# Starting a fused attention and feed-forward kernel with the value projection from scaled rows, and adding the shift's share at the end

## The chip, the cores and the metric

The kernel runs on one core of a Trainium2 chip. The metric is device time in microseconds (us) from the first to the last instruction of one execution, measured around the program. Before the change it is 832.6 us (median of 4 runs, 831.9 to 833.6). The profile is one further execution, recorded by the hardware profiler; its span is a little shorter than the time of that run (831.0 us in a run of 832.8). Runs here agree within about 0.3%, so differences of a microsecond are looked at in the trace and compared as ratios between runs of the same rounds on the same chip.

The engines are named as the profile names them: PE is the matmul engine (TensorE), DVE is VectorE, ACT is ScalarE, POOL is GpSimd, SP issues most of the DMA loads.

## The reference, cut to what matters

```python
x = A_x                                           # 2048 rows of 1024, bfloat16
mod = (silu(c) @ w_mod).reshape(1, 6, 1, 1024)     # c is one row; w_mod is 1024 x 6144
sa, ca, ga, sb, cb, gb = mod[:, 0], ..., mod[:, 5]

h = layernorm(x) * (1 + ca) + sa                   # scale and shift per column
q, k, v = split(h @ wqkv)                          # 32 heads of 32
phi(t) = where(t > 0, t + 1, exp(t)) + 1e-6
kv = einsum('bhsd,bhse->bhde', phi(k), v)          # summed over all rows
z  = einsum('bhsd->bhd', phi(k))
o  = (phi(q) @ kv) / (phi(q) . z + 1e-6)
x  = x + ga * (o @ wo)
# then the same with sb, cb, gb around a SwiGLU feed-forward block of width 3584
```

The algebra that the change uses: with the scaled rows alone, hs = layernorm(x) * (1 + ca), the values are v = hs @ wv + sa @ wv. The second term is one row, the same for every row of x. Its share in kv is z times that row, so it can be added once, at the end.

## The kernel before

The 2048 rows are worked in four chunks of 512 rows (`sc` 0 to 3), each of four row tiles of 128. Per chunk the kernel computes K, V and Q with 512-column matmuls. After the first two of the eight K groups of the next chunk comes a block `kvp` of 128 narrow matmuls that adds phi(k) times v of the chunk before. Chunk 0 is special: scale and shift must first be computed from `w_mod`. The start, shortened:

```python
for st in range(STC - 1):            # row tiles 0 to 2
    load_x(st, nc.sync)
for k in range(DC // MP):            # scale and shift weights, 8 loads of 384 KB
    load_a(k, 1, nc.scalar if k == 0 else nc.sync)
    load_a(k, 0, nc.sync)
...                                  # wk, the rest of w_mod, wv, row tiles 4 to 7, wq
with in_order(nc.vector, nc.scalar, nc.gpsimd):
    ...                              # statistics, row matvec for scale and shift, transposes
    k_mms(0, gs, accs, 0, 5)         # K of chunk 0 starts here
    ...
    k_evac(0, gs, accs)              # phi on ACT and DVE, frees the accumulators
    k_evac(0, gs7, accs7)
    k_evac(0, gs8, accs8)
for sc in range(NSC):
    if sc > 0:
        k_phase(sc, 0, 2); kv_phase(sc - 1); k_phase(sc, 2, 4); ...
    v_phase(sc)
    if sc + 1 < NSC:                 # layernorm of the next chunk's four row tiles
        with tc.issue_after(last_on[nc.vector.engine] if sc == 0 else last_phi[-5].ins):
            ln1(sc + 1)
    if sc == 0:
        q_phase(0, 0, 6)
```

```python
def phi_to(dst, acc):                # evacuation of one K or Q accumulator
    e = ep.tile([P, NB], BF16, name="eb")
    nc.scalar.activation(out=e[:], in_=acc, func=ACT.Exp)
    nc.vector.tensor_scalar(out=e[:], in0=e[:], scalar1=1.0, scalar2=PHI_EPS, op0=ALU.min, op1=ALU.add)
    last_phi[0] = nc.vector.scalar_tensor_tensor(out=dst, in0=acc, scalar=0.0, in1=e[:], op0=ALU.max, op1=ALU.add)

def ln1_stats(sc, t):                # statistics of one row tile: needs the tile in SBUF
    x_sb = x_tiles.pop(sc * STC + t)
    mv = small.tile([P, STC, 2], F32, name="mv")
    bn(x_sb, mv[:, 0, :])            # two bn_stats and one bn_aggr on DVE
    rstd = rstd_of(mv, 1)
    return sc, t, x_sb, mv, rstd
```

There are four accumulators of the kind that `acc_a()` hands out, and a matmul group that uses one can only start when one is free: in the changed kernel PE waits 3.23 us for one. The order of instructions on each engine is decided by a scheduler when the kernel is built; `issue_after` and `in_order` restrict it. At run time DVE works through its list in order: in the changed kernel it stands idle for 3.82 us with finished work behind the wait.

## Time and profile before

| before | value | view |
|---|---|---|
| time | 832.6 us (831.9 to 833.6) | 4 runs |
| PE busy | 99% of the span | busy table |
| PE share of the chain of waits | 97% | chain |
| first K matmul | 15.59 us | timeline of PE |
| Q of chunk 0 starts | 44.49 us | timeline of PE |
| granted PE clock | 1.00 from 5.8 us on | clock records |

These lines are the busy row of the engines and the chain of work that ended last, by engine and by line (before). "L98" is the helper through which nearly all matmuls go.

```profile
PE 819.9 (99%) x4502; PEld 378.9 (46%) x4581; DVE 344.5 (41%) x659; ACT 168.5 (20%) x253; POOL 64.3 (8%) x166
...
PE 97%; DMA 2%; issue 1%; DVE 0%; ACTq 0%; SPq 0%
```

PE is the bound. The only part of the chain that is not PE lies at the start. This is the chain in order of time, before (columns: start in us, length in us, what):

```profile
1.33 6.07 DMA wme<-in_w_mod_dram
...
7.83 6.40 DMA wme<-in_w_mod_dram
...
14.28 0.51 PE mod_ps L98 x8
14.79 4.21 PE acc L98 x19
```

So the first 14.2 us wait for `w_mod`. After that PE does not pause. The timeline of PE, before (start, length, engine, line, operation, out<-in, shapes, count; a bracket would tell an idle time and what ended it):

```profile
15.59 6.64 PE L98 MATMUL acc<-wk,hT 128*128 128x512 bf16 x29
...
30.68 13.98 PE L98 MATMUL acc<-wv,hT 128*128 128x512 bf16 x63
44.49 13.98 PE L98 MATMUL acc<-hT,wq 128*128 128x512 bf16 x62
```

K, V and Q of chunk 0 follow each other without a bracket. Later, behind the second `kvp`, the line is

```profile
92.25 10.46 PE L98 MATMUL acc<-wk,hT 128*128 128x512 bf16 x47 [0.16 <-issue]
```

that is, K of chunk 2 goes on to its end without a gap above 0.16 us.

What DVE does while they run, before:

```profile
28.49 0.29 DVE L296 TENSOR_SCALAR eb<-eb 128x512 bf16<-128x512 bf16 x1 [2.74 <-ACT eb L295]
28.81 0.69 DVE L298 SCALAR_TENSOR_TENSOR pk<-acc,eb 128x512 bf16<-128x512 f32 x1
...
35.78 0.69 DVE L298 SCALAR_TENSOR_TENSOR pk<-acc,eb 128x512 bf16<-128x512 f32 x1
36.39 1.87 DVE L224 BATCH_NORM_STATS2 stats<-x_sb 128x6 f32<-128x512 bf16 x3
```

The eight evacuations of K (`pk<-acc,eb`) come first, and only then the statistics (`BATCH_NORM_STATS2`) of the next chunk's row tiles.

### The profile page before, as it was taken

How to read it: one execution, taken by the hardware profiler on the slowest of the kernel's cores; microseconds unless marked ns; L12 is line 12 of the kernel's file. 1: busy time of each engine (PE TensorE's matmuls, PEld its weight loads, DVE VectorE, ACT ScalarE, POOL GpSimd, SP SyncE). 2: the span in 40 equal slices, each digit the busy share in tenths (PEclk: the TensorE clock that was granted, in tenths of full speed). 3: DMA queues.
4: the chain of work that ended last, by engine and by line, in shares of the span. 5: the costliest groups of instructions: out<-in, count | busy, mean ns of one | idle time of the engine just before them, and what ended most of it. 6: DMA issues, size and time to landing. Idle time of an engine off the chain costs nothing.

```text
span 831.0 us, 11112 instructions
## 1 busy us (share of the span) xinstructions
PE 819.9 (99%) x4502; PEld 378.9 (46%) x4581; DVE 344.5 (41%) x659; ACT 168.5 (20%) x253; POOL 64.3 (8%) x166
## 2 busy tenths in 40 slices
PE   8999999999999999999999999999999999999998
PEld 4444444444444444444444444444444444444444
DVE  5758879786354335421111354111114431111122
ACT  3455343434111111101111010111111101111000
POOL 2101020120221101100000010000001100000000
PEclk9999999999999999999999999999999999999999
DMA  9893964149986735646343183763405529710011
GB/s 324 296 203 65 194 150 102 37 101 326 375 204 219 227 121 169 160 153 211 110 146 108 54 221 92 249 195 100 153 1 174 152 68 345 231 45 0 19 58 51
DMA packets 144100, 129.07 MB, mean 155 GB/s; under 512 B 58608, under 2 KB 124656, under 8 KB 143536
## 3 DMA queue, kind: packets, MB, share of 16 engines
q1 hardware_dynamic: 139968, 114.97, 46.8%
q0 software_dynamic: 3792, 12.98, 4.9%
q8 instruction: 36, 0.59, 0.3%
q10 hardware_dynamic: 288, 0.40, 0.1%
q14 instruction: 16, 0.13, 0.0%
HBM read 101.98 MB, written 12.72 MB: 138 GB/s over the span
## 4 chain that ended last, share of the span: by engine, by line
PE 97%; DMA 2%; issue 1%; DVE 0%; ACTq 0%; SPq 0%
PE acc L98 90%; PE a_ps L98 7%; DMA wme<-in_w_mod_dram 2%; PE kvp L98 1%; PE wf L98 0%; PE den L98 0%; PE mod_ps L98 0%; ACTq L126 0%; PE tp L101 0%; SPq L135 0%; DVE e L698 0%; DVE ob L701 0%
## 5 line engine op out<-in xcount | busy, mean ns | idle before, releaser
L98 PE MATMUL acc<-h2T,wgu 128*128 128x512 bf16 x1755 | 385.6, 379 | 1.9
L98 PEld LDWEIGHTS <-wgu 128*128 128x128 bf16 x1792 | 175.3, 98 | 211.3
L677 DVE TENSOR_TENSOR gu<-acc,e 128x512 bf16<-128x512 f32 x112 | 77.4, 691 | 289.9 <-PE acc L98 278.8
L98 PE MATMUL acc<-wd,gu 128*128 128x512 bf16 (+2 forms) x908 | 195.2, 372 | 0.9
L676 ACT ACTIVATE e<-acc 128x512 f32<-128x512 f32 x112 | 66.9, 597 | 374.8 <-PE acc L98 363.4
L98 PEld LDWEIGHTS <-gu 128*128 128x128 bf16 x924 | 89.3, 98 | 104.4
L98 PEld LDWEIGHTS <-hT 128*128 128x128 bf16 x512 | 49.6, 98 | 59.8 <-DVE hT L237 0.9
L698 DVE TENSOR_TENSOR e<-acc,gb_bc 128x512 f32<-128x512 f32 (+2 forms) x33 | 22.3, 675 | 131.5 <-PE acc L98 122.5
L98 PE MATMUL a_ps<-wo,pq 128*128 128x512 bf16 x250 | 56.9, 379 | 0.3
L98 PE MATMUL acc<-wk,hT 128*128 128x512 bf16 x251 | 56.4, 379 | 0.5 <-issue 0.3
L98 PE MATMUL acc<-hT,wq 128*128 128x512 bf16 x249 | 55.8, 379 | 0.7 <-issue 0.5
L98 PE MATMUL acc<-wv,hT 128*128 128x512 bf16 x249 | 55.5, 379 | 0.4
L295 ACT ACTIVATE eb<-acc 128x512 bf16<-128x512 f32 x64 | 37.9, 596 | 75.4 <-PE acc L98 73.3
L234 ACT ACTIVATE xn<-x,nmr,rstd 128x1024 bf16<-128x1024 f32 x16 | 19.9, 1241 | 126.0 <-POOL nmr L232 126.0
L98 PEld LDWEIGHTS <-pq 128*128 128x128 bf16 x256 | 25.0, 98 | 30.2
L645 POOL DMA_DIRECT2D x_scratch<-x x16 | 9.8, 615 | 373.8 <-DVE x L638 373.6
L98 PEld LDWEIGHTS <-wq 128*128 128x128 bf16 x256 | 24.6, 98 | 29.8 <-issue 0.9
L296 DVE TENSOR_SCALAR eb<-eb 128x512 bf16<-128x512 bf16 x64 | 18.3, 290 | 31.2 <-ACT eb L295 31.0
L218 POOL TENSOR_TENSOR rstd<-veps,neg_half 128x1 f32<-128x1 f32 x32 | 17.8, 557 | 102.3 <-DVE veps L216 92.3
L638 DVE TENSOR_TENSOR x<-a_ps,x_sb 128x512 f32<-128x512 f32 x32 | 22.1, 690 | 8.6 <-PE a_ps L98 7.9
L701 DVE TENSOR_TENSOR ob<-e,x1r 128x512 bf16<-128x512 f32 (+2 forms) x33 | 22.3, 675 | 1.0
L639 DVE BATCH_NORM_STATS2 stats<-x 128x6 f32<-128x512 f32 x32 | 22.1, 693 | 1.0
(92 smaller groups left out, 295.9 us busy)
## 6 DMA issues: line engine op xcount, KB each, us to landing
wgu<-in_B_w_gate_dram SPq DMA_DIRECT2D x28, 1024.0 KB, 7.5
wgu<-in_B_w_up_dram SPq DMA_DIRECT2D x28, 1024.0 KB, 8.1
x_sb<-in_A_x_dram SPq DMA_DIRECT2D x32, 256.0 KB, 5.5
x_scratch<-x POOLq DMA_DIRECT2D x16, 512.0 KB, 3.4
x1r<-x_scratch SPq DMA_DIRECT2D x31, 256.0 KB, 2.7
wd<-in_B_w_down_dram SPq DMA_DIRECT2D x7, 1024.0 KB, 6.3
rbc<-rden_scratch POOLq DMA_DIRECT2D x16, 256.0 KB, 5.5
out_dram<-ob SPq DMA_DIRECT2D x31, 128.0 KB, 1.7
```

The costliest lines, as they stand in the source:

```text
L98: return tc.keep_in_program_order(nc.tensor.matmul(out, lhsT=lhsT, rhs=rhs, start=start, stop=stop))
L218: nc.gpsimd.tensor_tensor(out=rstd[:, 0:n], in0=veps[:, 0:n], in1=neg_half[:].to_broadcast([P, n]), op=ALU.pow)
L234: nc.scalar.activation(out=dst, in_=src, func=ACT.Identity, bias=nmr[:], scale=rstd[:, 0:1])
L295: nc.scalar.activation(out=e[:], in_=acc, func=ACT.Exp)
L296: nc.vector.tensor_scalar(out=e[:], in0=e[:], scalar1=1.0, scalar2=PHI_EPS, op0=ALU.min, op1=ALU.add)
L638: nc.vector.tensor_tensor(out=x1[:, ns], in0=a_ps[:], in1=x_t[:, ns], op=ALU.add)
L639: nc.vector.bn_stats(out=stats[:, nb, :], in_=x1[:, ns])
L645: nc.gpsimd.dma_start(out=x1_dram[st * P:(st + 1) * P, :], in_=x1[:])
L676: nc.scalar.activation(out=sg[:], in_=ps[0][:], func=ACT.Silu)
L677: gm = nc.vector.tensor_tensor(out=guT[sc][f // GPT][:, f % GPT, :], in0=ps[1][:], in1=sg[:], op=ALU.mult)
L698: nc.vector.tensor_tensor(out=yt, in0=y_ps, in1=gb_bc[:, ns], op=ALU.mult)
L701: nc.vector.tensor_tensor(out=ob, in0=yt, in1=x1r, op=ALU.add)
```

## The change

The intent: K needs scale and shift before it can start, V of scaled rows needs the scale alone. So chunk 0 starts with V, on half of the scale and shift weights and on two row tiles instead of three; the shift is computed while V runs; K follows with the full rows. The shift's share of V is a single row, sa @ wv, computed near the end with 32 narrow matmuls (`vb`) and added to KV as z times that row, for chunk 0's rows only. The statistics of the start's row tiles move forward, and the row loads of chunks 2 and 3 are put behind the transposing loads ("turns") of the chunk before.

```diff
@@ loads
-    for k in range(DC // MP):
-        load_a(k, 1, nc.scalar if k == 0 else nc.sync)
-        load_a(k, 0, nc.sync)
-    ... wk, row tile 3, rest of w_mod, wv, row tiles 4 to 7, wq
+    for j in range(DC):
+        load_block(wca, wm_v, j, D, nc.scalar if j == 0 else nc.sync)
+    for cc in range(DC):
+        load_block(wv, wqkv_v, cc, 2 * D)
+        if cc in (0, 2):
+            load_x(2 + cc // 2, nc.sync)
+    for j in range(DC):
+        load_block(wsa, wm_v, j, 0)
+    load_x(STC, nc.sync)
+    for cc in range(DC):
+        load_block(wk, wqkv_v, cc, D)
+    for st in range(STC + 1, 2 * STC):
+        load_x(st, nc.sync)
+    ... wq
@@ start of chunk 0 (cut)
-        k_mms(0, gs, accs, 0, 5)
-        ...
-        k_evac(0, gs, accs)
-        k_evac(0, gs7, accs7)
-        k_evac(0, gs8, accs8)
+        for cc in range(4, DC):
+            scale_to(hs, hT, cc, 0, H)
+        st3 = ln1_stats(0, 3)
+        gs = k_groups[0:4]
+        v_mms(hs, gs, accs, 0, 6)
+        ...
+        mod_rows(0, 0, DC)                      # the shift
+        mod_turn(0, DC)
+        ...
+        modulate_all(hT, ca1T, saT)
@@ main loop
-        v_phase(sc)
+        if sc == 0:
+            k_phase(0, 0, 8)
+        else:
+            v_phase(sc)
@@
             for st in range((sc + 2) * STC, (sc + 3) * STC):
-                load_x(st, nc.sync)
+                with tc.issue_after(last_load[0].ins):
+                    load_x(st, nc.sync)
@@ end of the K and V part
-    nc.vector.tensor_copy(out=KVB, in_=kv_acc[:, :, 0:DH])
+    vb = acc_b("vb", (HG, DH))
+    for cc in range(DC):
+        row_matvec(vb[:].rearrange("p g e -> p (g e)"), sc32[:, cc, :], wv[cc // 4][:, cc % 4, :], cc == 0, cc == DC - 1)
+    ...
+    nc.vector.tensor_tensor(out=zb, in0=vb[:], in1=z0.to_broadcast([P, HG, DH]), op=ALU.mult)
+    nc.vector.tensor_tensor(out=KVB, in0=kv_acc[:, :, 0:DH], in1=zb, op=ALU.add)
```

(Cut: the helpers, the filler matmuls at the start, and a shift of later Q groups by one place.)

More of the change, by code (lines that the diff above doesn't have):

```diff
@@ L122, in load_x @@
         x_tiles[st] = x_sb
-    for st in range(STC - 1):
+    for st in range(2):
         load_x(st, nc.sync)
     nc.scalar.dma_start(out=c_sb[:], in_=c_v)
-    wk = [big("wk", [4, D]), big("wk", [4, D])]
-    A, MP = 6, 2
-    AW, BW = A * P, (DC - A) * P
-    wma = [big("wme", [MP, 2, AW]) for _ in range(DC // MP)]
-    wmb = big("wme", [DC, 2, BW])
-    def load_a(k, q, eng):
-        eng.dma_start(out=wma[k][:, :, q, :], in_=wm_v[:, k * MP:(k + 1) * MP, q * D:q * D + AW])
-    def load_b(q, lo, hi):
-        nc.sync.dma_start(out=wmb[:, lo:hi, q, :], in_=wm_v[:, lo:hi, q * D + AW:(q + 1) * D])
@@ L140, in load_k @@
-    def load_k(cc):
-        nc.sync.dma_start(out=wk[cc // 4][:, cc % 4, :], in_=wqkv_v[:, cc, D:2 * D])
-    for k in range(DC // MP):
-        load_a(k, 1, nc.scalar if k == 0 else nc.sync)
-        load_a(k, 0, nc.sync)
-    load_k(0)
-    load_k(1)
-    load_x(STC - 1, nc.sync)
-    for cc in range(2, A):
-        load_k(cc)
-    for q in (1, 0):
-        load_b(q, 0, DC // 2)
-        load_b(q, DC // 2, DC)
-    for cc in range(A, DC):
-        load_k(cc)
-    def load_w(view, lo, name):
-        ts = []
-        for h in range(2):
-            t = big(name, [4, D])
-            nc.sync.dma_start(out=t[:], in_=view[:, 4 * h:4 * h + 4, lo:lo + D])
-            ts.append(t)
-        return ts
@@ L165, with load_block @@
-    wv = load_w(wqkv_v, 2 * D, "wv")
-    for st in range(STC, 2 * STC):
+    wv = [big("wv", [4, D]) for _ in range(2)]
+    wca = [big("wme", [4, D]) for _ in range(2)]
+    wsa = [big("wme", [4, D]) for _ in range(2)]
+    wk = [big("wk", [4, D]) for _ in range(2)]
+    def load_block(tiles, view, cc, lo, eng=nc.sync):
+        eng.dma_start(out=tiles[cc // 4][:, cc % 4, :], in_=view[:, cc, lo:lo + D])
+    for j in range(DC):
+        load_block(wca, wm_v, j, D, nc.scalar if j == 0 else nc.sync)
@@ L167 @@
+    for cc in range(DC):
[8 more added lines that the diff above has]
+    for st in range(STC + 1, 2 * STC):
         load_x(st, nc.sync)
-    wq = load_w(wqkv_v, 0, "wq")
+    wq = [big("wq", [4, D]) for _ in range(2)]
+    for h in range(2):
+        nc.sync.dma_start(out=wq[h][:], in_=wqkv_v[:, 4 * h:4 * h + 4, 0:D])
@@ L174 @@
     base_t = ep.tile([P, NB], BF16, name="eb")
-    base = base_t[:, 0:A * 64].rearrange("p (i q r) -> p i q r", q=2, r=32)
-    nc.gpsimd.memset(base[:, :, 0, :], 0.0)
-    nc.gpsimd.memset(base[:, :, 1, :], 1.0)
+    MW = DC * DH
+    nc.gpsimd.memset(base_t[:, 0:MW], 1.0)
     scT = const.tile([P, DC], BF16, name="scT")
@@ L185 @@
     scr_t = ep.tile([P, NB], F32, name="e")
-    scr = scr_t[:, 0:A * 64].rearrange("p (i q r) -> p i q r", q=2, r=32)
-    sa0T, ca0T = scr[:, :, 0, 0], scr[:, :, 1, 0]
+    scr = scr_t[:].rearrange("p (q i r) -> p q i r", q=2, r=DH)
+    ca0T = scr[:, 1, :, 0]
     sbT = const.tile([P, DC], F32, name="sbT")
@@ L195 @@
     gb_bc = const.tile([P, D], BF16, name="gb_bc")
-    kvs = k8.tile([P, HG * (2 * DH + 1)], F32, name="kvs", tag="k8")
+    kvs = k8.tile([P, HG * (2 * DH + 2)], F32, name="kvs", tag="k8")
     kv_acc = kvs[:, 0:HG * (DH + 1)].rearrange("p (g e) -> p g e", e=DH + 1)
-    kvb = kvs[:, HG * (DH + 1):].bitcast(BF16)
+    z0 = kvs[:, HG * (2 * DH + 1):].unsqueeze(2)
+    kvb = kvs[:, HG * (DH + 1):HG * (2 * DH + 1)].bitcast(BF16)
     KVB = kvb[:, 0:HG * DH].rearrange("p (g e) -> p g e", e=DH)
@@ L268, in ln1, with by_group, row_matvec, mod_rows @@
             ln1_norm(*ln1_stats(sc, t))
-    def mod_rows_a(k):
-        for j in range(k * MP, (k + 1) * MP):
-            rows = wma[k][:, j % MP, :, :].rearrange("p q (i r) -> p i q r", r=P)
-            for g in range(4):
-                mm(mod_ps[32 * g:32 * g + 32, 0:A * 64], lhsT=sc32[:, j, :], rhs=rows[:, :, :, 32 * g:32 * g + 32],
-                   start=False, stop=(j == DC - 1))
-    def mod_turn(lo, hi):
-        nc.vector.transpose(out=scr_t[:, lo * 64:hi * 64], in_=mod_ps[:, lo * 64:hi * 64])
-    def mod_cols_b():
-        cb = mod_ps[:, NB - 2 * (DC - A):NB]
-        mm(cb, lhsT=ident[:], rhs=base_t[:, 32 - (DC - A):32 + (DC - A)], start=True, stop=False)
-        for q in (1, 0):
-            for j in range(DC):
-                for i in range(DC - A):
-                    col = q * (DC - A) + i
-                    mm(cb[:, col:col + 1], lhsT=wmb[:, j, q, i * P:(i + 1) * P], rhs=scT[:, j:j + 1],
-                       start=False, stop=(q == 0 and j == DC - 1 and i == DC - A - 1))
-        nc.vector.tensor_copy(out=sca[:, :, A:DC], in_=cb.rearrange("p (q i) -> p q i", q=2))
+    def by_group(rows, g):
+        return rows.rearrange("p (i r) -> p i r", r=P)[:, :, g * DH:(g + 1) * DH]
+    def row_matvec(out, lhsT, rows, start, stop):
+        for g in range(4):
+            mm(out[g * DH:(g + 1) * DH, :], lhsT=lhsT, rhs=by_group(rows, g), start=start, stop=stop)
+    def mod_rows(q, lo, hi):
+        for j in range(lo, hi):
+            row_matvec(mod_ps[:, q * MW:(q + 1) * MW], sc32[:, j, :], (wsa, wca)[q][j // 4][:, j % 4, :],
+                       q == 0 and j == 0, j == DC - 1)
+    def mod_turn(lo, hi):
+        nc.vector.transpose(out=scr_t[:, lo * DH:hi * DH], in_=mod_ps[:, lo * DH:hi * DH])
+    def scale_to(hs, hT, cc, lo, hi):
+        nc.vector.tensor_scalar(out=hs[:, cc, lo:hi], in0=hT[:, cc, lo:hi], scalar1=ca0T[:, cc:cc + 1], scalar2=None,
+                                op0=ALU.mult)
     last_phi = [None]
@@ L321, in k_phase, with v_mms, v_evac @@
             mod_step(int(k_groups.index(g) in K_STEPS[sc]))
+    def v_mms(hT, gs, accs, cc_lo=0, cc_hi=DC):
+        for cc in range(cc_lo, cc_hi):
+            for (t, nb), acc in zip(gs, accs):
+                mm(acc[:], lhsT=hT[:, cc, t * P:(t + 1) * P], rhs=wv[cc // 4][:, cc % 4, nb * NB:(nb + 1) * NB],
+                   start=(cc == 0), stop=(cc == DC - 1))
+    def v_evac(sc, gs, accs):
+        for (t, nb), acc in zip(gs, accs):
+            nc.scalar.copy(out=vs[sc][:, t * D + nb * NB:t * D + (nb + 1) * NB], in_=acc[:])
     def v_phase(sc):
@@ L326, in v_phase @@
         nc.gpsimd.memset(v[:, VT:], 1.0)
-        for t in range(STC):
-            for nb in range(NNB):
-                acc = acc_a()
-                for cc in range(DC):
-                    mm(acc[:], lhsT=hTs[sc][:, cc, t * P:(t + 1) * P],
-                                     rhs=wv[cc // 4][:, cc % 4, nb * NB:(nb + 1) * NB],
-                                     start=(cc == 0), stop=(cc == DC - 1))
-                nc.scalar.copy(out=v[:, t * D + nb * NB:t * D + (nb + 1) * NB], in_=acc[:])
+        for g in k_groups:
+            acc = acc_a()
+            v_mms(hTs[sc], [g], [acc])
+            v_evac(sc, [g], [acc])
     def q_phase(sc, lo=0, hi=DC, steps=0):
@@ L360, in kv_phase @@
             nc.vector.tensor_copy(out=kv_acc, in_=kvv)
+            nc.vector.tensor_copy(out=z0, in_=kv_acc[:, :, DH:DH + 1])
         else:
@@ L478, in keep_warm_f32 @@
             mm(acc[:, 0:zeros.shape[1]], lhsT=zeros[:, 0:P], rhs=zeros, start=True, stop=True)
-    gs = k_groups[0:6]
-    accs = [acc_a() if i < 4 else acc_b("acc") for i in range(6)]
-    spare = accs[5]
+    accs = [acc_a() for _ in range(4)]
+    spare = accs[3]
     keep_warm_f32(spare, 3)
@@ L485 @@
     hT = hTs[0] = big("hT", [DC, SCW])
-    pks[0] = big("pk", [STC, D])
-    H = 3 * P
+    hs = big("hs", [DC, SCW])
+    vs[0] = big("v", [VT + DH])
+    nc.gpsimd.memset(vs[0][:, VT:], 1.0)
+    H = 2 * P
     with in_order(nc.vector, nc.scalar, nc.gpsimd):
         mod_ps = acc_b("mod_ps")
-        mm(mod_ps[:, A * 64:A * 64 + DC], lhsT=c_sb[:], rhs=ident[0:DC, 0:DC], start=True, stop=True)
+        mm(mod_ps[:, 0:DC], lhsT=c_sb[:], rhs=ident[0:DC, 0:DC], start=True, stop=True)
         for g in range(4):
-            mm(mod_ps[32 * g:32 * g + 32, 0:A * 64], lhsT=ident[:, 0:32], rhs=base_t[:, 0:A * 64],
-               start=True, stop=False)
-        nc.scalar.activation(out=scT[:], in_=mod_ps[:, A * 64:A * 64 + DC], func=ACT.Silu)
-        st0 = ln1_stats(0, 0)
-        nc.vector.tensor_copy(out=sc32[:], in_=scT[:].unsqueeze(2).to_broadcast([P, DC, 32]))
-        xns = [ln1_norm(*st0)] + [ln1_norm(*ln1_stats(0, t)) for t in range(1, 3)]
-        keep_warm_f32(spare, 3)
-        mod_rows_a(0)
-        pe_transpose_tile(hT, xns[0], 0)
+            mm(mod_ps[g * DH:(g + 1) * DH, MW:2 * MW], lhsT=ident[:, 0:DH], rhs=base_t[:, 0:MW], start=True, stop=False)
+        nc.scalar.activation(out=scT[:], in_=mod_ps[:, 0:DC], func=ACT.Silu)
+        xn0 = ln1_norm(*ln1_stats(0, 0))
+        st1 = ln1_stats(0, 1)
+        nc.vector.tensor_copy(out=sc32[:], in_=scT[:].unsqueeze(2).to_broadcast([P, DC, DH]))
+        xn1 = ln1_norm(*st1, dve=True)
+        keep_warm_f32(spare, 1)
         for h in range(2):
@@ L505 @@
             nc.scalar.copy(out=sc_row[:, h * NB:(h + 1) * NB], in_=accs[h][:])
-        mod_rows_a(1)
-        pe_transpose_tile(hT, xns[1], 1)
-        keep_warm(spare, 2)
-        pe_transpose_tile(hT, xns[2], 2)
-        mod_rows_a(2)
-        keep_warm(spare, 5)
-        mod_rows_a(3)
-        keep_warm(spare, 4)
-        mod_turn(0, 1)
-        modulate(hT, 0, ca0T, sa0T, 0, P)
-        modulate(hT, 0, ca0T, sa0T, P, H)
-        mod_turn(1, A)
-        for cc in range(1, A):
-            modulate(hT, cc, ca0T, sa0T, 0, H)
@@ L520 @@
-        nc.vector.tensor_copy(out=sca[:, :, 0:A], in_=scr[:, :, :, 0].rearrange("p i q -> p q i"))
-        k_mms(0, gs, accs, 0, 5)
-        xn3 = ln1_norm(*ln1_stats(0, 3), dve=True)
-        pe_transpose_tile(hT, xn3, 3)
-        for cc in range(A):
-            modulate(hT, cc, ca1T, saT, H, SCW)
-        k_mms(0, gs, accs, 5, A)
-        mod_cols_b()
-        gs7, accs7 = k_groups[6:7], [acc_b("acc")]
-        k_mms(0, gs7, accs7, 0, A)
-        for cc in range(A, DC):
-            modulate(hT, cc, ca1T, saT)
@@ L532 @@
-        k_mms(0, gs + gs7, accs + accs7, A, DC)
-        gs8, accs8 = k_groups[7:8], [acc_b("acc")]
-        k_mms(0, gs8, accs8)
-        k_evac(0, gs, accs)
-        k_evac(0, gs7, accs7)
-        k_evac(0, gs8, accs8)
+        keep_warm(spare, 3)
+        mod_rows(1, 0, 3)
+        pe_transpose_tile(hT, xn0, 0)
+        keep_warm(spare, 3)
+        mod_rows(1, 3, 5)
+        pe_transpose_tile(hT, xn1, 1)
+        keep_warm(spare, 3)
+        mod_rows(1, 5, DC)
+        keep_warm(spare, 3)
+        mod_turn(DC, DC + 1)
@@ new lines @@
+        scale_to(hs, hT, 0, 0, H)
+        mod_turn(DC + 1, 2 * DC)
+        for cc in range(1, 4):
+            scale_to(hs, hT, cc, 0, H)
+        xn2 = ln1_norm(*ln1_stats(0, 2))
+        for cc in range(4, DC):
+            scale_to(hs, hT, cc, 0, H)
+        st3 = ln1_stats(0, 3)
+        gs = k_groups[0:4]
+        v_mms(hs, gs, accs, 0, 6)
+        pe_transpose_tile(hT, xn2, 2)
+        for cc in range(DC):
+            scale_to(hs, hT, cc, H, H + P)
+        xn3 = ln1_norm(*st3)
+        v_mms(hs, gs, accs, 6, DC)
@@ new lines @@
+        gs2, accs2 = k_groups[4:6], [acc_b("acc") for _ in range(2)]
+        v_mms(hs, gs2[0:1], accs2[0:1])
+        v_evac(0, gs, accs)
+        pe_transpose_tile(hT, xn3, 3)
+        for cc in range(DC):
+            scale_to(hs, hT, cc, H + P, SCW)
+        v_mms(hs, gs2[1:2], accs2[1:2])
+        mod_rows(0, 0, DC)
+        mod_turn(0, DC)
+        nc.vector.tensor_copy(out=sca[:], in_=scr[:, :, :, 0])
+        v_evac(0, gs2, accs2)
+        for g in k_groups[6:8]:
+            acc = acc_a()
+            v_mms(hs, [g], [acc])
+            v_evac(0, [g], [acc])
@@ L538 @@
+        modulate_all(hT, ca1T, saT)
+        nc.vector.tensor_copy(out=sc32[:], in_=saT.unsqueeze(2).to_broadcast([P, DC, DH]))
     with tc.issue_after(last_on[nc.gpsimd.engine]):
@@ L587 @@
     kv_phase(NSC - 1)
-    nc.vector.tensor_copy(out=KVB, in_=kv_acc[:, :, 0:DH])
+    vb = acc_b("vb", (HG, DH))
+    for cc in range(DC):
+        row_matvec(vb[:].rearrange("p g e -> p (g e)"), sc32[:, cc, :], wv[cc // 4][:, cc % 4, :], cc == 0, cc == DC - 1)
     nc.vector.tensor_tensor(out=Zden[:], in0=kv_acc[:, :, DH:DH + 1].to_broadcast([P, HG, DH]),
                             in1=zmask[:], op=ALU.mult)
+    zb_t = ep.tile([P, NB], F32, name="e")
+    zb = zb_t[:, 0:HG * DH].rearrange("p (g e) -> p g e", e=DH)
+    nc.vector.tensor_tensor(out=zb, in0=vb[:], in1=z0.to_broadcast([P, HG, DH]), op=ALU.mult)
+    nc.vector.tensor_tensor(out=KVB, in0=kv_acc[:, :, 0:DH], in1=zb, op=ALU.add)
     def fold_wo(h, nb):
@@ L600, in fold_wo @@
             (nc.scalar.copy if g % 2 == 0 else nc.vector.tensor_copy)(out=wo[h][:, g, ns], in_=ps[g][:])
-    q_phase(1, 2, 4)
+    q_phase(1, 2, 5)
     tpk = acc_b("tp", (2, P), BF16)
@@ L606 @@
     nc.vector.tensor_copy(out=KVT, in_=tpk[:])
-    q_phase(1, 4, 5)
+    q_phase(1, 5, 6)
     den_sum(0, acc_a())
@@ L610 @@
     den_spread(0)
-    q_phase(1, 5, 7)
+    q_phase(1, 6, 8)
     fold_wo(0, 1)
-    q_phase(1, 7, 8)
-    q_phase(2, 0, 1)
+    q_phase(2, 0, 2)
     fold_wo(1, 0)
-    q_phase(2, 1, 3)
+    q_phase(2, 2, 4)
     fold_wo(1, 1)
@@ L705, in down @@
                         side.pop(0)()
-    q_phase(2, 3, 4)
+    q_phase(2, 4, 5)
     with tc.issue_after(last_phi[0].ins):
@@ L710 @@
     with tc.issue_after(applied.ins):
-        q_phase(2, 4, 6)
+        q_phase(2, 5, 7)
     for st in range(STC):
         wo_tile(st)
-    q_phase(2, 6, 8)
+    q_phase(2, 7, 8)
     nc.vector.tensor_scalar_add(out=cb1T[:], in0=cbT[:], scalar1=1.0)
```

## The prediction

> **What bounds it now.** One core, clock 1.00 throughout, so TensorE is the bound: PE is 99% busy (busy table) and 97% of the chain of waits. The timeline shows its stream unbroken (gaps of at most 0.16 us) from the first K matmul at 15.59 us to the end, one 512-column matmul per 0.216 us. Only the first 15.6 us can shrink: the chain there is two weight DMAs (`wme`, 1.33 to 7.40 and 7.83 to 14.23 us), then 1.4 us of row matvec, turn and modulate. After 15.59 us only added PE work or a new stall counts.
>
> **What the change does.** Before, K of chunk 0 needs scale and shift: 3 row tiles and 3.1 MB of `w_mod`, 3.9 MB in all. After, V needs the scale alone: two row tiles and 2.1 MB, 2.6 MB. Landings before come in order of issue, 0.66 us per 256 KB once warm[...]. 2.6 MB had landed at about 10.9 us, so the first V matmul should come at about 11.9 us: 3.7 us earlier (estimate from those landings and the 1.36 us from last landing to first matmul before).
>
> From there 128 matmuls (27.6 us), two sets of transposes (0.9), the shift's row matvec (1.0; the `mod_ps` group of 8 took 0.44), some 0.3 us waiting on `wv`. Without a stall chunk 0's Q would start at about 41.8 us instead of 44.5: 2.7 us gained. Late in the kernel the vector times V weights (`vb`, 32 narrow matmuls, about 1.0 us) is new PE work on the chain. The removed column matvec (0.9 us) is already counted. The DVE work for z0, zb and KVB hides behind Q groups, of which one more stands before the transposes. Gain so far: 1.7 us, about 831.1.
>
> **A new stall.** The instruction order of the two programs shows what the diff does not. Before, the statistics of the next four row tiles stand on DVE after all eight K evacuations. After, the first statistics of row tile 7 stand before the first K evacuation, and that tile is the last of the start's loads, behind 2 MB of `wq`. Before it landed at 39.2 us; after, with the same 12.6 MB but no 512-byte pieces, I estimate 36.2 us. DVE is in order, so no K accumulator is freed until about 2.0 us later (0.65 statistics, 2 x 0.29, 0.65, waits): 38.2 us. There are four; K starts at about 28.0 us and its fifth group wants one at 34.9 us. PE stalls some 3.3 us. Q then starts at about 45.1 us, 0.6 later than before, plus 1.0 for `vb`.
>
> **Predicted: 834.4 us**, range 830.8 to 837.5. Faster by over 2%: 0.01; within 2%: 0.98; slower by over 2%: 0.01.
>
> **What would show it.** Right: first V matmul at 11.5 to 12.5 us; in the timeline one PE gap of 2 to 5 us in the middle of chunk 0's K matmuls, at 34 to 39 us, with DVE idle before a BATCH_NORM_STATS2 released by DMA `x_sb`; exp activations idle behind it; `vb` about 1.0 us at around 150 us; no other PE gap.
> Wrong: DVE not waiting on `x_sb` in chunk 0's K, or PE unbroken there; then about 831.
>
> **What would make me wrong.** The last row tile landing before 33 us removes the stall[...]. `wv` or `wk` late would stall V or K earlier, but hide within the same wait. A long gap might lower the clock, a few us more.

(Two passages are cut. One was a remark on the order of landings. The old trace shows that order: the loads that SP issued in the first 29 us, as far as their landings are recorded, landed in their order of issue, four of 256 KB in a row at 14.91, 15.59, 16.26 and 16.94 us. The other said how late tile 7 might land at worst, 38 us, with a stall of 5 us. It rested on the lag of the landings behind the data in the old trace, 1.3 us at 14 us and 2.7 us at 28 us, and on a cause for it that was not shown. Neither is a term of the sum, which stays 831.1 plus 3.3 for the stall: 834.4 us. As to the 512-byte pieces: while they ran in the kernel before, from 18 to 22 us, the DMA engines moved 283 to 344 GB/s, and from 24 to 28 us, without them, 387 to 393.)

## The result, and the profile after

| | before | after |
|---|---|---|
| time, median of 4 runs | 832.6 us (831.9 to 833.6) | 836.8 us (835.9 to 838.7) |
| ratio after / before | | 1.0052 (95%: 1.0032 to 1.0072) |
| span of the profiled run | 831.0 us | 834.8 us |

A ratio here and below is the mean time of one kernel's runs over the mean of the other's runs of the same rounds, so it is not quite the ratio of the medians. The change made the kernel slower by half a per cent: the same, by a threshold of 2%, but clear of noise. Predicted were 834.4 us with a range of 830.8 to 837.5.

The page's same lines, after:

```profile
PE 821.0 (98%) x4530; PEld 379.4 (45%) x4609; DVE 349.0 (42%) x679; ACT 168.5 (20%) x253; POOL 64.0 (8%) x165
...
PE 94%; DMA 4%; issue 1%; DVE 0%; ACTq 0%; SPq 0%
```

PE's share of the chain fell from 97% to 94% and DMA's rose from 2% to 4%: more of the span now waits for data, although less data is needed to start. The timeline of PE, after:

```profile
12.05 5.35 PE L98 MATMUL acc<-wv,hs 128*128 128x512 bf16 x24
...
23.41 1.06 PE L98 MATMUL mod_ps<-wme,sc 128*32 128x256 bf16 x32
...
27.86 7.07 PE L98 MATMUL acc<-wk,hT 128*128 128x512 bf16 x32
38.16 1.44 PE L98 MATMUL acc<-wk,hT 128*128 128x512 bf16 x3 [3.23 <-DVE pk L279]
39.82 6.70 PE L98 MATMUL acc<-wk,hT 128*128 128x512 bf16 x28 [0.22 <-issue]
46.35 13.98 PE L98 MATMUL acc<-hT,wq 128*128 128x512 bf16 x63
```

V starts at 12.05 us, 3.5 us ahead of the old K. But after 32 K matmuls, four groups, PE is idle for 3.23 us until DVE has evacuated a K accumulator. The next 32 matmuls take from 38.16 to 46.35 us, 8.2 us instead of 6.9. DVE, after, at that time:

```profile
32.46 0.14 DVE L199 TENSOR_SCALAR veps<-mv 128x1 f32<-128x1 f32 x1
36.42 0.69 DVE L207 BATCH_NORM_STATS2 stats<-x_sb 128x6 f32<-128x512 bf16 x1 [3.82 <-DMA x_sb<-in_A_x_dram]
37.03 0.48 DVE L277 TENSOR_SCALAR eb<-eb 128x512 bf16<-128x512 bf16 x2
37.42 1.28 DVE L279 SCALAR_TENSOR_TENSOR pk<-acc,eb 128x512 bf16<-128x512 f32 x2
```

DVE is idle too, for 3.82 us, waiting for a row tile (`x_sb`, tile 7), while finished K accumulators stand behind that wait. Two things that the diff hides put it there. In the listing of the kernel before, `ln1` is held only behind the last DVE instruction of the `in_order` block. That was the last K evacuation; the change moved K out of the block, so the anchor is now a copy at 27.80 us, and the scheduler set the statistics ahead of the first K evacuation. And although the load of tile 7 stands ahead of `wq` in the program, in SP's list it comes behind both `wq` loads:

```profile
25.85 1.09 SPq L151 DMA_DIRECT2D wq<-in_A_wqkv_dram  x2
27.24 0.34 SPq L121 DMA_DIRECT2D x_sb<-in_A_x_dram  x1
```

The chain, after, tells of the same wait in one stretch (start, length, what):

```profile
27.24 9.16 DMA x_sb<-in_A_x_dram
...
36.42 0.69 DVE stats L207
37.11 0.39 DVE eb L277 x2
37.51 0.61 DVE pk L279
...
38.16 1.44 PE acc L98 x3
```

There is a second loss, at 97 us, which the chain can only call "issue". Timeline of PE, after (`kvp` is the block of narrow matmuls that adds phi(k) times v):

```profile
92.60 1.22 PE L98 MATMUL kvp<-v,pk 128*32 128x64 bf16 x128
93.98 2.10 PE L98 MATMUL acc<-wk,hT 128*128 128x512 bf16 x9 [0.16 <-issue]
97.40 1.89 PE L98 MATMUL acc<-wk,hT 128*128 128x512 bf16 x8 [1.31 <-issue]
```

PE stops for 1.31 us, ten matmuls behind `kvp`, with no semaphore to wait for.

The starts of a few stages put the losses in place (us, from the profiled runs; "mended" is the experiment x7_stats_late below):

| stage | before | after | after minus before | mended |
|---|---|---|---|---|
| first projection matmul | 15.59 (K) | 12.05 (V) | -3.54 | |
| Q of chunk 0 | 44.49 | 46.35 | +1.86 | 41.72 |
| first kvp | 61.85 | 63.71 | +1.86 | 59.08 |
| second kvp | 90.87 | 92.60 | +1.73 | 87.96 |
| third kvp | 119.91 | 122.95 | +3.04 | 117.33 |
| Q behind the fourth kvp and `vb` | 150.18 | 154.10 | +3.92 | 148.25 |
| end of the span | 831.0 | 834.8 | +3.8 | 829.2 |

(In the last but one row the first matmul's record is missing in the traces before and after, but not in the mended one, so those two read 0.2 us late; their difference stands.)

The sum, worked out from these lines: 3.54 gained at the start; 3.23 lost in the stall; 1.28 lost in the slow matmuls behind it (8.19 less 6.91 for 32 matmuls at 0.216); 0.89 more for the other work between (one more set of transposes, the shift's matvec; it is the rest of the +1.86, and 0.72 of it lies in the V stretch, 15.81 us against 15.09 for K before); 0.13 regained before the second `kvp`; 1.31 lost at 97 us; 0.88 for `vb` (3.92 less 3.04). Nothing else moves by more than 0.2 us in the remaining 680 us.

### The profile page after: what moved, and what is told of

Its sections match the earlier page's. It is cut to its first block, busy times and chain, and to the rows that moved or that the text cites. A ratio compares the mean times of both kernels' runs of the same rounds, so it can differ in the third digit from the quotient of the medians.

```text
span 834.8 us, 11201 instructions
## 1 busy us (share of the span) xinstructions
PE 821.0 (98%) x4530; PEld 379.4 (45%) x4609; DVE 349.0 (42%) x679; ACT 168.5 (20%) x253; POOL 64.0 (8%) x165
## 4 chain that ended last, share of the span: by engine, by line
PE 94%; DMA 4%; issue 1%; DVE 0%; ACTq 0%; SPq 0%
PE acc L98 87%; PE a_ps L98 7%; DMA wme<-in_w_mod_dram 2%; DMA x_sb<-in_A_x_dram 1%; DMA wk<-in_A_wqkv_dram 1%; DMA wv<-in_A_wqkv_dram 1%; PE kvp L98 1%; PE wf L98 0%; PE den L98 0%; PE vb L98 0%; DVE stats L207 0%; DVE pk L279 0%; ACTq L126 0%; DVE eb L277 0%; DVE e L704 0%
## 5 line engine op out<-in xcount | busy, mean ns | idle before, releaser
L98 PEld LDWEIGHTS <-hT 128*128 128x128 bf16 x448 | 43.9, 99 | 58.1 <-issue 6.8
L98 PE MATMUL acc<-wv,hT 128*128 128x512 bf16 x186 | 41.6, 379 | 0.3
L207 DVE BATCH_NORM_STATS2 stats<-x_sb 128x6 f32<-128x512 bf16 x32 | 20.9, 670 | 6.8 <-DMA x_sb<-in_A_x_dram 6.8
```

Of the source, the lines that this page charges most:

```text
L98: return tc.keep_in_program_order(nc.tensor.matmul(out, lhsT=lhsT, rhs=rhs, start=start, stop=stop))
L207: nc.vector.bn_stats(out=stats[:, i, :], in_=src[:, i * NB:(i + 1) * NB])
```

## The experiments

Ten runs, each with a profile. All results passed the check against the reference, even `no_vb`, which leaves out most of the shift's share; so that check cannot tell whether this term is added rightly. The kernel before was timed again in the rounds of each call (medians 833.4, 833.5 and 833.4 us on three chips), and ratios are to those. A ratio of one call beside that of another compares different chips, each against its own kernel before.

**Theory A**: DVE works in order; the statistics of row tile 7 stand ahead of the first K evacuation, and that tile is loaded last. Its rival **B**: the gap has to do with late weights, or with how the accumulators are freed after V.

### x7_before_wq: the same order on DVE, but the tile comes earlier

```diff
-    for h in range(2):
-        nc.sync.dma_start(out=wq[h][:], in_=wqkv_v[:, 4 * h:4 * h + 4, 0:D])
 ... (behind the in_order block:)
+    for h in (0, 1):
+        with tc.issue_after(last_load[0].ins):
+            nc.sync.dma_start(out=wq[h][:], in_=wqkv_v[:, 4 * h:4 * h + 4, 0:D])
```

(A first form of this edit, and of the next, left the `wq` loads at their place in the program and ordered them with `issue_after` only; it deadlocked when it was built.)

> The changed kernel with one thing moved: row tile 7 is loaded ahead of the two 1 MB wq loads; the instruction order on DVE stays the same. Theory A (K of chunk 0 stalls because DVE, in order, waits for row tile 7 ahead of the first K evacuation): the tile lands at about 31.2 us, not 36.4; the PE gap of 3.2 us at 38.2 us is gone, and with it the 1.4 us of half-speed matmuls after it; chunk 0's Q starts at about 41.7 us instead of 46.35; total 836.8 - 4.7 = about 832.1 us. Rival B (the gap comes from late weights or from the accumulators that ScalarE empties after V): the gap stays near 3 us, total about 836.8.

Measured: 831.8 us (830.8 to 832.2), ratio 0.9979 (0.9964 to 0.9994). K of chunk 0 runs unbroken and Q starts at 42.0 us:

```profile
28.21 13.98 PE L98 MATMUL acc<-wk,hT 128*128 128x512 bf16 x64
42.02 6.21 PE L98 MATMUL acc<-hT,wq 128*128 128x512 bf16 x28
```

Moving one 256 KB load ahead of two of 1 MB took away stall and slow matmuls. B falls: the weights, and the accumulators after V, are as before.

### x7_between_wq: half the dose

```diff
-    for h in range(2):
-        nc.sync.dma_start(out=wq[h][:], in_=wqkv_v[:, 4 * h:4 * h + 4, 0:D])
+    nc.sync.dma_start(out=wq[0][:], in_=wqkv_v[:, 0:4, 0:D])
 ... (behind the in_order block:)
+    for h in (1,):
+        with tc.issue_after(last_load[0].ins):
+            nc.sync.dma_start(out=wq[h][:], in_=wqkv_v[:, 4 * h:4 * h + 4, 0:D])
```

> Dose: row tile 7 between the two wq loads, DVE order the same. Theory A: it lands at about 33.8 us, and the fifth K group starts some 2 us later, at 35.6 us, so a gap of 0.7 to 1.0 us; if a gap this short leaves the clock alone, Q starts at about 42.5 us and the total is about 832.9 us. Rival B: gap near 3 us, total 836.8.

Measured: 832.7 us (832.2 to 833.3), ratio 0.9994 (0.9978 to 1.0011). The tile landed at 34.05 us, and the gap is as long as the arithmetic said:

```profile
27.69 7.24 PE L98 MATMUL acc<-wk,hT 128*128 128x512 bf16 x32
35.81 7.07 PE L98 MATMUL acc<-wk,hT 128*128 128x512 bf16 x32 [0.88 <-DVE pk L278]
```

Landing at 36.39, 34.05 and about 31.3 us gives gaps of 3.23, 0.88 and 0. (The third is an estimate, as its record is missing: the row tile before it landed at 30.60 us, 0.67 us after the one before. DVE took the tile up at 32.60 us without waiting.) The clock stayed at 1.00: 32 matmuls behind the short gap took 6.9 us.

### x7_stats_late: the same late load, but another order on DVE ("the mended kernel")

```diff
         for t in range(STC):
-            ln1_norm(*ln1_stats(sc, t))
+            if sc == 1 and t == STC - 1:
+                with tc.issue_after(last_phi[-5].ins):
+                    st = ln1_stats(sc, t)
+            else:
+                st = ln1_stats(sc, t)
+            ln1_norm(*st)
```

> The changed kernel with the loads as they are (row tile 7 lands last, about 36.4 us), but its statistics ordered on DVE behind the fourth K evacuation. Theory A (the order on DVE is the cause, not the transfer): no gap in K of chunk 0, Q starts at about 41.7 us, total about 832.1 us. If the late transfer itself holds PE by some other way, the gap stays and the total is 836.8.

Measured: 831.05 us (830.9 to 831.3), ratio 0.9972 (0.9957 to 0.9987). The tile lands as late as ever (36.8 us), and DVE takes it up when four evacuations are done:

```profile
37.50 0.69 DVE L284 SCALAR_TENSOR_TENSOR pk<-acc,eb 128x512 bf16<-128x512 f32 x1
38.11 0.68 DVE L207 BATCH_NORM_STATS2 stats<-x_sb 128x6 f32<-128x512 bf16 x1
```

K of chunk 0 runs unbroken, and Q starts at 41.72 us, as the prediction had it for a kernel without the stall (41.8):

```profile
27.91 13.98 PE L98 MATMUL acc<-wk,hT 128*128 128x512 bf16 x64
41.72 6.64 PE L98 MATMUL acc<-hT,wq 128*128 128x512 bf16 x30
```

So the stall takes both, the late load and the place on DVE; mending either is enough. With the stall gone the idea of the change pays, by a quarter of a per cent.

### before_early: the same fault put into the kernel before

```diff
+        early = ln1_stats(1, 3)
         k_evac(0, gs, accs)
 ...
-            ln1_norm(*ln1_stats(sc, t))
+            ln1_norm(*(early if sc == 1 and t == 3 else ln1_stats(sc, t)))
```

> The kernel before with one thing moved: the statistics of row tile 7 ahead of the eight K evacuations on DVE. Its row tile 7 landed at 33.5 us (the load at 39.2 us is tile 8's, a reading of mine in the prediction that was wrong). Theory A: evacuation starts at 35.1 us instead of 28.5; V, which needs the first accumulator, starts at about 36.2 us instead of 30.7, a PE gap of about 5.5 us; total 832.6 + 5.5 = 838 us, up to 3 us more if the clock drops after it. Rival: an accumulator is freed another way, no gap, 832.6.

Measured: 840.5 us (839.6 to 841.2), ratio 1.0080 (1.0066 to 1.0094). DVE was idle for 6.78 us and PE for 4.39 us; the tile landed at 32.2 us here, 1.3 us before what I took from the old profile, which is why the gap is 4.4 and not 5.5 us.

```profile
32.25 1.29 DVE L224 BATCH_NORM_STATS2 stats<-x_sb 128x6 f32<-128x512 bf16 x2 [6.78 <-DMA x_sb<-in_A_x_dram]
...
34.95 16.47 PE L98 MATMUL acc<-wv,hT 128*128 128x512 bf16 x64 [4.39 <-DVE pk L298]
```

The 64 V matmuls took 16.3 us (34.95 to 51.26) instead of 13.8: another 2.5 us in slow matmuls.

### stall_filled: are the slow matmuls the clock?

Theory G: PE's clock is lowered because PE was idle. Fifteen matmuls on zeros go where the stall was.

```diff
         for g in k_groups[lo:hi]:
+            if sc == 0 and g == k_groups[4]:
+                keep_warm(acc_b("acc"), 15)
             accs = [acc_a()]
```

> The changed kernel with 15 matmuls on zeros (3.2 us) put where PE stalls. Theory G (after the stall the clock is lowered for some us: 32 K matmuls took 8.2 us in the changed kernel and 9.8 in another run, instead of 6.9): no gap, the clock stays at 1.00, the four K groups behind it take 6.9 us, Q starts at about 45.0 us instead of 46.35, total about 1.4 us below the changed kernel, 835.4. If the slow matmuls come from data or accumulators arriving late, they stay slow and the total is 836.8.

Measured: 835.4 us (834.7 to 835.5), ratio 1.0018 (1.0004 to 1.0031), where the changed kernel has 1.0052. Timeline of PE, stall_filled:

```profile
34.84 3.40 PE L98 MATMUL acc<-sel 128*128 128x512 bf16 x15
38.24 7.09 PE L98 MATMUL acc<-wk,hT 128*128 128x512 bf16 x32
45.16 5.13 PE L98 MATMUL acc<-hT,wq 128*128 128x512 bf16 x23
```

The K groups still had to wait until 38.2 us, but then took 6.9 us. So the second part of the loss was the clock. In the changed kernel the windows view shows it (columns: window, us, busy time of PE, PEld, DVE, ACT, POOL, then granted PE clock, DMA share, GB/s):

```profile
36.00:38.00 2.00, 0.00 (x0) 0.00 (x0) 1.58 (x4) 0.00 (x0) 0.00 (x0) 0.85 0.91 201
38.00:40.00 2.00, 1.62 (x4) 0.69 (x5) 1.91 (x8) 0.00 (x0) 0.42 (x1) 0.50 0.00 0
40.00:42.00 2.00, 2.00 (x8) 0.78 (x7) 0.77 (x2) 1.48 (x2) 1.23 (x5) 0.80 0.01 4
```

The clock records give the lengths at half clock: 3.41 us in the changed kernel (37.40 to 40.81), 6.83 us, twice as long, in rows_undone and in before_early, none in stall_filled or x7_between_wq. So in the changed kernel PE worked at half clock from 38.16 to 40.81 us; 2.65 us at half clock lose 1.3 us, and 1.28 us were measured. In the 3.41 us before the clock fell PE had been idle for 2.47 us in the changed kernel, 2.05 us in rows_undone, 2.65 us in before_early and 2.72 us in late_sb. In the profiled runs the PE gaps of 3.23 us (changed kernel), 3.30 us (rows_undone), 4.39 us (before_early) and 3.07 us (late_sb) lowered the clock; those of 0.88 us (x7_between_wq), 1.31 us (changed kernel, at 97 us) and 1.22 us (stall_filled) did not. Gaps of 3.23 and 3.30 us cost 1.3 us in one run and 2.7 us in another (below): the first reached 0.76 us into the stretch at half clock, the second 1.26 us, and the second stretch was twice as long. Why was not shown; no run tests it. The runs of the changed kernel with a mean clock of 1.000, 0.998, 0.998 and 0.995 took 835.9, 836.6, 837.0 and 838.7 us: the same order. A fall of 3.41 us lowers the mean to 0.998, so in the first of these runs the clock did not fall, with the same kernel.

### rows_undone: does the stop at 97 us come from the moved row loads?

**Theory C**: the row loads that were put behind the transposes push the next transposing loads of `w_mod` later, onto PE's instruction fetch (the page of the changed kernel has a DMA queue of kind "instruction", with 36 packets and 0.59 MB). Its rival **D**: it comes from elsewhere.

```diff
-                with tc.issue_after(last_load[0].ins):
-                    load_x(st, nc.sync)
+                load_x(st, nc.sync)
```

> The changed kernel with its last part undone: the row loads of chunks 2 and 3 interleave with the transposing loads again, as before. Theory C (the 1.3 us PE gap at 97.4 us, for which no semaphore shows, comes from the moved row loads, which push the transposing w_mod loads 4 us later, onto PE's instruction fetch): that gap is gone, the stall at 38 us stays; total about 835.5 us. Rival D (the gap comes from elsewhere, for instance from PE being 1.7 us later against the same transfers, or from chance): gap and total unchanged, 836.8 us.

Measured: 838.0 us (837.4 to 838.9), ratio 1.0056 (1.0041 to 1.0071): no faster. The stop is still there, shorter, at the same place ten matmuls behind the second `kvp`, and K of chunk 2 has a new wait of 0.64 us for ACT. The stall of chunk 0 is there as expected (3.30 us), with 6.83 us at half clock instead of 3.41, so that the four groups behind it took 9.6 us (38.21 to 47.84). C falls: the stop does not need that part of the change. Whether the moved loads lengthen it (1.31 against 0.53 us) is not shown, since two profiles of one and the same mended kernel have 0.21 and 0.63 us (below).

The stop turned out to be in nearly every profile. The trace's DMA records hold packets of 16 KB on the queue of kind "instruction" (36 in the whole run), and one belongs to each of these places. The page after has 4530 matmuls and 4609 weight loads on PE, 254 to a packet; in the trace before, from 276 to 825 us, a packet starts after every 253 of these records on average, where some records are missing (us; read from the packet and matmul records):

```
run             kvp starts   packet            PE resumes   gap
before             90.87     91.03 to  91.95       -        under 0.2
after              92.60     94.89 to  96.05     97.40      1.31
x7_before_wq       88.27     90.39 to  91.33     92.96      1.21
x7_between_wq      88.97     90.40 to  91.42     92.94      0.36
x7_stats_late      87.96     89.39 to  90.40     91.78      0.21
rows_undone        95.65     97.03 to  98.12     99.66      0.53
no_vb              87.91     90.24 to  91.25     92.54      1.15
mended_again       87.81     89.62 to  90.79     92.05      0.63
stall_filled       91.41     90.97 to  92.20     93.81      1.22
before_early       98.08     99.03 to 100.21    101.67      0.97
```

PE resumes 1.3 to 1.6 us after the packet's end, in every run that has a gap. At the first and third `kvp` of these runs the packet starts 0.1 to 2.5 us before `kvp` does, and there is no gap. The best evidence is stall_filled, made for another purpose: its 15 extra matmuls, each with its weight load, put 30 instructions more into PE's list, and the gap came 30 instructions earlier: not ten matmuls (20 instructions) behind `kvp` but five (10 instructions) before its end.

```profile
91.41 1.18 PE L98 MATMUL kvp<-v,pk 128*32 128x64 bf16 x123
93.81 0.22 PE L98 MATMUL kvp<-v,pk 128*32 128x64 bf16 x5 [1.22 <-issue]
```

So the gap belongs to a place in PE's instruction list, not to any data. By these counts a packet stands for about 254 of PE's instructions (an estimate: 9139 records over 36 packets), and `kvp` alone is 256 (128 matmuls and 128 weight loads) in 1.2 us. **Theory F**: PE waits there for its packet, and the packet is late because of the transposing loads in flight.

### late_sb: the transposing loads pushed behind the second kvp

On top of the mended kernel:

```diff
-            k_phase(sc, 2, 4)
+            k_phase(sc, 2, 3)
+            if sc == 2:
+                last_load[0] = mod_load(3, sbT, True)   # held back by a DVE write
+            k_phase(sc, 3, 4)
 ... (the eight wo loads move behind ln1(3); mod_load(3, sbT) at sc == 1 is taken out)
```

> The mended kernel (row tile 7's statistics behind the fourth K evacuation), with the second pair of transposing w_mod loads held back on DVE until the third K group of chunk 2, and the wo loads behind the next transposes. Theory F (the small PE gap 10 matmuls after the second kvp block is PE waiting for its next block of instructions, whose fetch is delayed by the transposing loads): the 16 KB packet of the instruction queue starts before or at the start of kvp instead of 1.4 us after it, and the gap there (0.2 to 1.4 us in five runs so far) is gone; total 0.2 to 0.9 us below the mended kernel, about 830.5 us where before is 832.8, unless the transposes pushed back make K of chunk 3 wait. If the gap has another cause it stays at 10 matmuls after kvp.

Measured: 835.2 us (834.0 to 836.0), ratio 1.0014 (1.0000 to 1.0027): slower than the mended kernel, and yet the clearest sign for F. At the second `kvp` (87.64 us) the packet now runs from 86.60 to 87.52 us, ahead of `kvp`, and there is no gap. At the third, where the `wo` loads that I had moved were now in flight (the last landed at 123.19 us), the packet runs from 120.29 to 121.67 us, 3.7 us after the start of `kvp`, and PE stands:

```profile
117.70 2.33 PE L98 MATMUL acc<-wk,hT 128*128 128x512 bf16 x10
123.10 3.38 PE L98 MATMUL acc<-wk,hT 128*128 128x512 bf16 x9 [3.07 <-issue]
```

This gap too lowered the clock for 3.41 us. I had moved the fault from one `kvp` to the next. It was not transposing loads this time but the plain `wo` loads, so F should say loads in flight, not transposing loads only.

### early_sb and mended_again: the loads brought forward instead

On top of the mended kernel, `mod_load(3, sbT, True)` stands between the third and fourth K group of chunk 1 (not 2), and the `wo` loads stay where they were. The loads then run from 65.3 us, where the queue was idle. mended_again is the mended kernel once more, in the same rounds.

> The mended kernel with the second pair of transposing w_mod loads not pushed back but brought forward: held on DVE until the third K group of chunk 1 (about 64 us), so that they run in the idle time of the queue before the transposes of chunk 2. Theory F (PE's instruction fetch is delayed by transposing loads in flight): no transposing w_mod load runs at 85 to 95 us, the 16 KB instruction packet at the second kvp starts about 1 us before kvp, the gap 10 matmuls after it (0.2 to 1.4 us) is gone, and no other kvp has one; total 0.2 to 1.3 us below the mended kernel of the same rounds: about 830.3 us where that one has 831.1. Rival: the gap there does not depend on these loads and stays.

> A repeat of the mended kernel (row tile 7's statistics behind the fourth K evacuation) on the same chip and in the same rounds, to compare with: ratio to before about 0.997, total about 831.1 us, a gap of 0.2 to 1.4 us 10 matmuls after the second kvp.

Measured: early_sb 830.7 us (830.5 to 831.1), ratio 0.9968 (0.9955 to 0.9982); mended_again 831.2 us (831.1 to 831.4), ratio 0.9975 (0.9963 to 0.9988). In early_sb the packet at the second `kvp` (88.53 us) runs from 87.57 to 88.78 us and the gap is gone; the other two blocks of K have none either:

```profile
89.91 9.44 PE L98 MATMUL acc<-wk,hT 128*128 128x512 bf16 x43 [0.16 <-issue]
```

mended_again has its gap at the same place:

```profile
92.05 7.28 PE L98 MATMUL acc<-wk,hT 128*128 128x512 bf16 x33 [0.63 <-issue]
```

The times are 0.5 us apart in their means. The intervals of the ratios overlap, but no run of early_sb took longer than the shortest of mended_again (831.07 us each). The packets at the first `kvp` tell the same by dose, though no run was made for them. They belong to the same place in PE's list in all kernels with the changed start except stall_filled. Where the DMA share (windows view) was 0.03 to 0.05 in the 2.5 us before `kvp` (after, x7_before_wq, x7_between_wq, rows_undone), the packet started 1.3 to 1.6 us ahead of `kvp`; at 0.72 to 0.90 (early_sb, late_sb, x7_stats_late) 0.7 to 1.0 us ahead; at 1.26 and 1.31 (mended_again, no_vb) only 0.1 us ahead. early_sb is the fastest of the kernels that leave nothing out, and faster than before by 0.3%.

### no_vb: what the vector times V weights costs

The mended kernel with 4 of the 32 `vb` matmuls. Its output is wrong, which doesn't matter for the time.

```diff
-    for cc in range(DC):
-        row_matvec(vb[:]..., sc32[:, cc, :], wv[cc // 4][:, cc % 4, :], cc == 0, cc == DC - 1)
+    for cc in range(1):
+        row_matvec(vb[:]..., sc32[:, cc, :], wv[cc // 4][:, cc % 4, :], True, True)
```

> The mended kernel with 28 of the 32 matmuls of the vector times V weights left out; the result is wrong on purpose. Prediction of the cost of that part of the change: 0.86 us for 8 groups of four, so about 0.75 us less than the mended kernel (831.05 beside a before of 833.4), ratio to before about 0.9963. If the part hid in a wait of PE, no change.

Measured: 830.6 us (830.2 to 831.0), ratio 0.9962 (0.9949 to 0.9974), against 0.9972 and 0.9975 of the mended kernel in its two calls. The difference, 0.10 to 0.13% or about 0.8 to 1.1 us, is of the expected size, but the intervals overlap, so the time alone does not prove it; nor were the gaps at the second `kvp` equal (1.15 us in the profile here, 0.21 and 0.63 us in the two of the mended kernel). The stage table has 0.88 us for it.

## Why the prediction was right, and where it was not

- *"2.6 MB had landed at about 10.9 us, so the first V matmul should come at about 11.9 us."* The last of these weights landed at 10.16 us and the first V matmul came at 12.05. Both near, but for different reasons: the loads were 0.7 us faster, and PE did not use it, because filler matmuls and transposes stood ahead of the matvec until 10.89 us.
- *"Without a stall chunk 0's Q would start at about 41.8 us."* The mended kernel: 41.72 us.
- *"PE stalls some 3.3 us"*, K from 28.0, fifth group due at 34.9, accumulator at 38.2 us. Measured: 27.86, idle from 34.93, 38.16; 3.23 us. x7_before_wq, x7_between_wq, x7_stats_late and before_early show the cause from four sides.
- *"Before it landed at 39.2 us"* is wrong. The load at 39.2 us is row tile 8; tile 7 landed at 33.5 us, ahead of `wq`. The change did two things to tile 7, where I saw one: it put its load behind `wq` as well as its statistics ahead of K. The estimate of 36.2 us for after (36.39 measured) survives, because it counts the bytes ahead of the tile in the new order.
- *`vb` "about 1.0 us"*: 0.88 us.
- *"A long gap might lower the clock, a few us more"* stood among the doubts and not in the sum. It cost 1.28 us in the profiled run; with it Q starts at 46.35 instead of 45.1 us. This is one of two terms that were mis-sized.
- *"No other PE gap"* is the step that failed: 1.31 us behind a late instruction packet at 97 us, 0.2 to 1.3 us in other runs. I did not think of the instruction packets. In the kernel before, the packet starts 0.16 us after the same `kvp`, without a gap above 0.2 us; in x7_stats_late it starts 1.43 us after it, with a gap of 0.21 us. How late it may start without a gap was not shown.

834.4 plus 1.3 for the clock and 1.3 for the stop at 97 us, less 0.1 for `vb` and some rounding, is the measured 836.8. The range held; the mechanism named for most of it was shown.

What stays open: by which queue or engine loads in flight delay the packet, and why so unequally: the packet starts 0.16 us after the second `kvp` in the kernel before and 3.74 us after the third in late_sb. The traces show that they do (late_sb, early_sb and the packets at the first `kvp`), not how.

## What to carry to other kernels

When work is moved to an earlier place, look at what now stands in front of the work that frees the bottleneck's buffers, in the list of an engine that works in order (here DVE, idle for 3.82 us): one statistic that waits for one late 256 KB load held four finished accumulators, and the fix was to move either by a few places. A PE gap of 3 us can cost 4 to 6 us, because the clock can come down with it (here 3.23 us cost 4.5 and 3.30 us cost 6.0), and large loads in flight near a block of many tiny matmuls (here 256 instructions in 1.2 us) can leave PE waiting for instructions (here 0.2 to 1.3 us, once 3.07 us). A shorter start is worth only what the next stage does not give back, so follow the stage starts, not the first matmul.
